# Retention followed by a gated MLP on one core: zero products planned by recent stream, four ranks shifted, and another order of loads and tiles

## The chip, the core and the metric

The kernel runs on one core of a Trainium2 chip. The metric is the device time of one execution in microseconds; before the change it is 212.71 us, the median of three runs (212.57 to 212.76). The engines are named as in the profile: PE (TensorE), DVE (VectorE), ACT (ScalarE), POOL (GpSimd) and SP, whose queue issues the loads. [...]

## What is computed

```python
for t in range(S):                                   # 4 batches, 8 heads, S = 768, D = 64
    state = gamma * state + einsum('bhd,bhe->bhde', k[t], v[t])
    y[t] = einsum('bhd,bhde->bhe', q[t], state) / sqrt(D)
x = y transposed to (B, S, 512)
gate = sigmoid(causal depthwise convolution of x with conv_w, 5 taps)
out = (gate * (x @ w_val)) @ w_out                   # both weights 512 x 512, float32
```

## The kernel before

**Chunks.** The sequence is cut into 6 chunks of 128 tokens for each of 4 batches: 24 chunks g, the four batches of a sequence chunk behind each other. For each chunk TensorE makes scores (k against q), multiplies them by a mask on DVE into `u`, adds k-by-v products to a running state `z_ps` (copied out by ACT as `snap`), and makes y from `u` and from the state before. DVE moves y out of PSUM times a decay (`evac`, L510) into `x`. The first four chunks have no state before them: `first_scores` (L370), `first_mask` (L402), `first_y` (L447) and `first_state` (L414) do them; POOL's `decay` (L346) scales v or k before the state products.

**The MLP.** When all four batches of a sequence chunk are there, ACT rounds x to `xh` (`round_x`, L520), POOL makes the rest `xl` (`rest_x`, L525), and a value tile takes 12 products of 512 columns (`val`, L616: wvh by xh, wvl by xh, wvh by xl). The gate takes one tap on ACT (L599), four on DVE (L601) and a sigmoid (L608); `gated` (L631, DVE) multiplies the two, ACT rounds the product (L638), POOL makes its rest (`rest_gv`, L642), and an output tile takes 12 products (`outp`, L650), a copy by ACT (L660) and a store. There are 24 value tiles and 24 output tiles. The weights arrive as 64-bit floats and each quarter is converted: two ACT passes (L550, L569), two DVE passes (L554, L560), a POOL sum (L573), an ACT rounding (L583) and a POOL rest (L587).

**The order** of every engine's instructions comes from `plan`, a list scheduler that runs when the program is built. Each step has a due time, given by the string `WORK`: `p` the table of positions, `s`, `y`, `z` scores, y and state of the next of the first four chunks, `h` the scores and half state of the first later chunk, `v` the attention of the next later chunk, `w` load and conversion of the next quarter of w_out, `V` a value tile with its gate, `O` an output tile. A backward pass turns due times into ranks; the engine that is free first takes, of its steps whose inputs are there by the planner's own table of durations, the one with the lowest rank. The tuple `LOADS` sets the due times of the first transfers on SP's queue: `q`, `v`, `k` of a chunk's parts (q with transposed k, v, natural k), `a` the first three quarters of a chunk at once, `t` the table `small` (masks, decays), `w` a quarter of w_val.

**Zero products.** While the first value tile has not begun, `plan` puts products of zeros (`filler`, L679) into TensorE's planned rests, so that its clock is held up. Before the change a rest of given length gets `FILLED`, 0.55, of its length in fillers of 0.46 us, whatever ran earlier.

In what follows s0 to s3, y0 to y3 and z0 to z3 are scores, y and state of the first four chunks; a1 to a3 and k1 to k3 their transfers; w0 to w3 the quarters of w_val; V1 the first value tile, O1 the first output tile.

## Time and profile before

| what | before |
|---|---|
| median of 3 runs | 212.71 us |
| the profiled execution, its own time | 214.2 us |
| its span, first to last instruction | 212.4 us |
| PE busy | 200.8 us, 95% |
| DVE, ACT, POOL busy | 123.7, 110.2, 105.7 us |
| mean granted TensorE clock | 0.991 |
| moved by DMA | 36.25 MB |

The span is one execution; 1.8 us of its own time lies outside it. A row of the timeline gives the start and length of a group of instructions, the engine, the line of the kernel, what it writes and reads, how many it holds, and in brackets how long the engine was idle before it and which event ended that. The table by windows gives for each stretch the busy time of the engines, the mean granted clock of TensorE, the share of the DMA engines and the rate in GB/s.

### The profile page before, as it was taken

The page shows a single profiled execution, that of the slowest core. Times are in us where ns is not written, and L with a number is a line of the kernel's source. Part 1 is how long each engine was busy: PE and PEld are TensorE (multiplying, and loading weights), DVE is VectorE, ACT ScalarE, POOL GpSimd, SP SyncE. Part 2 cuts the span into 40 slices and gives each one's busy share as a digit, 9 for nine tenths or more (in the row PEclk, how much of TensorE's full clock was granted, in tenths as well). Part 3 has the DMA queues.
Part 4 walks back from the last instruction along what each step waited for, and adds up shares of the span by engine and source line. Part 5 has one row for each costly group of instructions (what it writes and reads, how often), then busy time and mean ns, then how long its engine had stood idle before and what let it go on. Part 6 is the DMA issues. An engine that isn't in the chain of part 4 may idle for free.

```text
span 212.4 us, 7838 instructions
## 1 busy us (share of the span) xinstructions
PE 200.8 (95%) x3502; PEld 159.9 (75%) x3502; DVE 123.7 (58%) x189; ACT 110.2 (52%) x237; POOL 105.7 (50%) x93
## 2 busy tenths in 40 slices
PE   8648899899999999999999999999999999999992
PEld 3437777678878888788887888788787688878782
DVE  0456999982189922899228992226796269911100
ACT  2655868793568344675447655146364445423221
POOL 0158999999942682535736424626142352204200
PEclk9996999999999999999999999999999999999999
DMA  5999997627575506717476137448111100120122
GB/s 166 367 416 416 360 345 329 201 56 288 176 285 201 204 0 243 257 32 243 179 245 207 49 73 275 153 143 299 62 49 52 52 3 0 70 81 1 48 99 102
DMA packets 9254, 36.25 MB, mean 171 GB/s; under 512 B 1154, under 2 KB 1538, under 8 KB 6660
## 3 DMA queue, kind: packets, MB, share of 16 engines
q1 hardware_dynamic: 5472, 29.43, 39.0%
q10 hardware_dynamic: 3748, 6.32, 8.0%
q8 instruction: 27, 0.44, 0.9%
q14 instruction: 7, 0.06, 0.1%
HBM read 29.46 MB, written 6.29 MB: 168 GB/s over the span
## 4 chain that ended last, share of the span: by engine, by line
PE 77%; DVE 7%; ACT 2%; DMA 1%; issue 1%; DVEq 0%; ACTq 0%
PE mm L650 32%; PE mm L616 27%; PE sy L430 11%; PE sy L357 4%; DVE acc L601 4%; PE z_ps L414 4%; DMA out_dram<-o_sb 1%; DVE top L560 1%; DVE gate L631 1%; DVE acc L554 1%; ACT gate L608 1%; ACT o_sb L660 0%; ACT acc L599 0%; ACT acc L550 0%; DVE x L510 0%
## 5 line engine op out<-in xcount | busy, mean ns | idle before, releaser
L601 DVE SCALAR_TENSOR_TENSOR acc<-x,cw_sb,acc 128x512 f32<-128x512 f32 x96 | 66.8, 750 | 2.8 <-ACT acc L599 2.3
L525 POOL TENSOR_TENSOR xl<-x,xh 128x512 fp32r<-128x512 f32 x24 | 30.8, 1285 | 40.9 <-ACT xh L520 40.8
L642 POOL TENSOR_TENSOR gvl<-gate,gvh 128x512 fp32r<-128x512 f32 x24 | 31.0, 1291 | 31.5 <-ACT gvh L638 31.5
L650 PE MATMUL mm<-woh,gvl 128*128 128x512 f32 (+1 forms) x100 | 38.8, 396 | 0.0
L650 PE MATMUL mm<-woh,gvh 128*128 128x512 f32 (+1 forms) x100 | 38.5, 392 | 0.1
L650 PE MATMUL mm<-wol,gvh 128*128 128x512 f32 (+1 forms) x100 | 37.9, 387 | 0.0
L616 PE MATMUL mm<-xl,wvh 128*128 128x512 f32 x96 | 34.5, 399 | 0.0
L346 POOL TENSOR_TENSOR att<-att,small_sb 128x512 f32<-128x512 f32 x24 | 25.0, 1045 | 15.5 <-DMA att<-in_att_dram 15.5
L616 PE MATMUL mm<-xh,wvh 128*128 128x512 f32 x96 | 32.0, 399 | 0.0
L631 DVE TENSOR_TENSOR gate<-mm,gate 128x512 f32<-128x512 f32 x24 | 16.5, 688 | 20.1 <-PE mm L616 17.8
L616 PE MATMUL mm<-xh,wvl 128*128 128x512 f32 x96 | 27.0, 397 | 0.0
L379 DVE TENSOR_TENSOR u<-sy,small_sb 128x512 f32<-128x512 f32 x20 | 13.7, 687 | 21.5 <-PE sy L357 21.5
L638 ACT CAST gvh<-gate 128x512 fp32r<-128x512 f32 x24 | 14.8, 619 | 21.8 <-DVE gate L631 21.8
L660 ACT COPY o_sb<-mm 128x512 f32<-128x512 f32 (+1 forms) x25 | 14.2, 569 | 18.6 <-PE mm L650 17.4
L510 DVE TENSOR_TENSOR x<-sy,dec 128x512 f32<-128x512 f32 x20 | 13.7, 684 | 17.4 <-PE sy L357 15.3
L650 PEld LDWEIGHTS mm<-woh,gvh 128*128 128x128 f32 x100 | 18.8, 188 | 5.2 <-issue 0.6
L520 ACT CAST xh<-x 128x512 fp32r<-128x512 f32 x24 | 14.8, 618 | 14.2 <-DVE x L510 13.3
L650 PEld LDWEIGHTS mm<-woh,gvl 128*128 128x128 f32 x100 | 18.6, 188 | 4.7 <-POOL gvl L642 0.7
L608 ACT ACTIVATE gate<-acc 128x512 f32<-128x512 f32 x24 | 14.4, 599 | 13.9 <-DVE acc L601 7.6
L650 PEld LDWEIGHTS mm<-wol,gvh 128*128 128x128 f32 x100 | 18.7, 188 | 3.8
L616 PEld LDWEIGHTS mm<-xl,wvh 128*128 128x128 f32 x96 | 18.0, 188 | 4.4
L616 PEld LDWEIGHTS mm<-xh,wvl 128*128 128x128 f32 x96 | 17.9, 188 | 4.3
(51 smaller groups left out, 249.5 us busy)
## 6 DMA issues: line engine op xcount, KB each, us to landing
att<-in_att_dram SPq DMA_DIRECT2D x20, 1024.0 KB, 5.4
out_dram<-o_sb ACTq DMA_DIRECT2D x23, 256.0 KB, 2.0
wst<-in_w_dram SPq DMA_DIRECT2D x8, 512.0 KB, 9.3
att<-in_att_dram SPq DMA_DIRECT2D x3, 768.0 KB, 9.5
att<-in_att_dram SPq DMA_DIRECT2D x5, 256.0 KB, 12.0
att<-in_att_dram SPq DMA_DIRECT2D x1, 512.0 KB, 4.2
out_dram<-o_sb ACTq DMA_DIRECT2D x2, 128.0 KB, 1.7
small_sb<-in_small_dram SPq DMA_DIRECT2D x1, 68.0 KB, 4.2
```

Source lines behind the costliest of these rows:

```text
L346: nc.gpsimd.tensor_tensor(v, v, vd_sb[:, c, :].unsqueeze(2).broadcast_to([P, 8, HALF]), op=ALU.mult)
L430: nc.tensor.matmul(sy[cols, h, off:off + HALF], lhsT=lhsT, rhs=rhs, start=start, stop=True, skip_group_check=True,)
L520: nc.scalar.copy(xh[n][:, :, b], xs[n][:, :, b, HALO:])
L525: nc.gpsimd.tensor_tensor(xl[n][:, :, b], xs[n][:, :, b, HALO:], xh[n][:, :, b].bitcast(F32), op=ALU.subtract)
L601: nc.vector.scalar_tensor_tensor(acc, x[:, :, k:k + P], cw_sb[:, m, k:k + 1], acc, op0=ALU.mult, op1=ALU.add,)
L608: nc.scalar.activation(gate[n, m], accs.pop((n, m)), AF.Sigmoid)
L616: nc.tensor.matmul(vps[n, m], lhsT=w[:, m, ct * P:(ct + 1) * P], rhs=xx[n][:, ct].rearrange("p b t -> p (b t)"), start=(i == 0), stop=(i = ...
L631: nc.vector.tensor_tensor(gv, vps.pop((n, m)), gv, op=ALU.mult)
L638: nc.scalar.copy(gvs[n, m][0], gate[n, m])
L642: engine.tensor_tensor(gvl, gate.pop((n, m)), gvh.bitcast(F32), op=ALU.subtract)
L650: nc.tensor.matmul(ops[n, b, cs.start][:, 0:cs.stop - cs.start], lhsT=gg[:, b * P:(b + 1) * P], rhs=w[:, ct, cs], start=(i == 0), stop=(i ...
L660: nc.scalar.copy(o_sb[:, 0:step], ops.pop((n, b, cs.start))[:, 0:step])
```

## The change

Fillers are planned by another rule. `plan` keeps a list of what TensorE has streamed (`streamed`: 1024 for a filler, 512 for a large product, 32 for each small one, 48 in the first scores and y). In front of each TensorE step with a rest before it, it sums what began in the last `WINDOW`, 3.41 us, and adds as many fillers as lack to `FLOOR`, 4400, at most 0.85 of the rest. Four steps get another rank after the backward pass: `rest_x` of chunk 0, batch 0, `rest_gv` of tile (0, 2) and the first sigmoid (which loads ACT's table) later, `evac` of chunk 2 earlier. The first transfers and the tiles come in another order: a2 is moved ahead of w1, k1 ahead of w1, and k2 and k3 ahead of a3, and the table `small` behind v; in `WORK` the states and attention steps stand earlier among the first tiles, w_out's quarters are spread, and the string ends in five output tiles instead of four.

```diff
-FILL, FILLED = 0.46, 0.55
+FILL, FILLED = 0.46, 0.85
+WINDOW, FLOOR = 3.41, 4400
+LATER = {
+    ("rest_x", 0, 0): 4.98,
+    ("rest_gv", 0, 2): 2.53,
+    ("first_sigmoid",): 1.59,
+    ("evac", 2): -0.60,
+}
@@ in plan, behind the backward pass
+    for s in steps:
+        s.rank += LATER.get((s.fn.__name__, *(a for a in s.args if isinstance(a, int))), 0.0)
@@
+    streamed = []
@@ ahead of a TensorE step
-            for i in range(int((start - since) * FILLED / FILL) if filling else 0):
+            done_lately = sum(w for t, w in streamed if t > start - WINDOW)
+            wanted = max(0, ceil((FLOOR - done_lately) / (2 * P * 4)))
+            for i in range(min(wanted, int((start - since) * FILLED / FILL)) if filling else 0):
                 f = Step(0, "PE", FILL, [], [], filler, (ring,))
...
+                streamed.append((f.start, 2 * P * 4))
...
         if e == "PE":
+            streamed.append((start, 32 * s.small * s.wide + 512 * s.big))
...
-    LOADS = (("q", 0), ("t", 0), ("k", 0), ("v", 0), ("w", 0), ("a", 1), ("w", 1), ("a", 2), ("a", 3), ("k", 1), ("w", 2), ("k", 2), ("k", 3), ("w", 3))
+    LOADS = (("q", 0), ("k", 0), ("v", 0), ("t", 0), ("w", 0), ("a", 1), ("a", 2), ("k", 1), ("w", 1), ("k", 2), ("k", 3), ("a", 3), ("w", 2), ("w", 3))
...
-        "spysysszyyzzzVwwVwwhvVVOOvvOvOVvVvVVOvOvVVO"
-        "vvVOvVvOVVOvOvVVOvvOVOvVOOvvvVVOVOOVVOVOOOO"
+        "spsysyysyzwzzVwhzVVwvvwVOvOOvvOVvVvVVOvOVvV"
+        "vVVvOOvOOVVvOVvOvVOvOVvVVOVOvvvVOVOVVOVOOOOO"
```

## The prediction

> **What bounds the kernel now.** I began with the page: its span, TensorE's busy time, the clock by slices, and the chain of work that ended last.

> ```profile
> span 212.4 us, 7838 instructions
> PE 200.8 (95%) x3502; PEld 159.9 (75%) x3502; DVE 123.7 (58%) x189; ACT 110.2 (52%) x237; POOL 105.7 (50%) x93
> PEclk9996999999999999999999999999999999999999
> PE 77%; DVE 7%; ACT 2%; DMA 1%; issue 1%; DVEq 0%; ACTq 0%
> ```

> TensorE is the bound on the whole, but an average hides where it isn't. The table by windows shows that.

> ```profile
> 10.00:15.00 5.00, 2.63 (x68) 1.83 (x67) 2.77 (x6) 2.59 (x8) 2.67 (x3) 1.00 1.02 418
> 15.00:20.00 5.00, 3.60 (x70) 2.81 (x74) 2.90 (x4) 3.04 (x7) 3.21 (x3) 0.73 1.05 415
> 20.00:25.00 5.00, 4.17 (x110) 3.73 (x104) 4.58 (x7) 3.53 (x7) 5.00 (x6) 0.93 0.96 369
> 25.00:35.00 10.00, 10.00 (x146) 7.77 (x145) 9.92 (x16) 7.63 (x16) 10.00 (x9) 1.00 0.98 374
> 35.00:45.00 10.00, 9.45 (x236) 7.33 (x236) 9.63 (x16) 7.75 (x17) 10.00 (x10) 1.00 0.44 151
> 45.00:206.00 161.00, 160.60 (x2767) 129.80 (x2757) 91.76 (x139) 80.14 (x176) 73.59 (x61) 1.00 0.39 136
> ```

> After the stretch, the columns are busy time of PE, weight loads, DVE, ACT and POOL, then clock, DMA share and GB/s. From 45 to 206 us PE idles 0.40 of 161 us: another order of tiles can win at most that there, and can lose more. From 10 to 25 us the DMA engines are full (0.96 to 1.05) while PE, DVE and POOL have rests: the loads set the pace. From 25 to 45 us PE, DVE and POOL are all nearly full. So the end of the kernel is the moment at which TensorE turns dense, plus the work then left. The timeline of PE shows the moment.

> ```profile
> 11.50 0.90 PE L370 MATMUL sy<-att 64*64 64x128 f32 x32 [1.29 <-DMA att<-in_att_dram]
> ...
> 13.47 0.90 PE L447 MATMUL ye<-u,att 64*64 64x128 f32 x32 [0.45 <-DVE u L402]
> 16.23 0.90 PE L370 MATMUL sy<-att 64*64 64x128 f32 x32 [1.85 <-DMA att<-in_att_dram]
> 17.30 1.22 PE L679 MATMUL ye<-const-float32-0.0 128*128 128x256 f32 x2 [0.17 <-DVE x L510]
> 18.45 1.55 PE L370 MATMUL sy<-att 64*64 64x128 f32 x32
> 19.79 1.27 PE L447 MATMUL ye<-u,att 64*64 64x128 f32 x32
> 21.88 0.90 PE L447 MATMUL ye<-u,att 64*64 64x128 f32 x32 [0.82 <-DVE x L510]
> ...
> 23.35 0.69 PE L414 MATMUL z_ps<-att 64*64 64x64 f32 x32
> 23.98 1.16 PE L679 MATMUL sy<-const-float32-0.0 128*128 128x128 f32 x8
> 25.07 0.69 PE L414 MATMUL z_ps<-att 64*64 64x64 f32 x32
> 25.69 1.20 PE L616 MATMUL mm<-xh,wvh 128*128 128x512 f32 x4
> 26.82 0.69 PE L414 MATMUL z_ps<-att 64*64 64x64 f32 x32
> ```

> These are s1, y1, s2, a filler, s3, y2, y3, z1, fillers, z2, V1 and z3. V1 begins at 25.69; from there on PE is dense, and z3 is still to do. V1 needs the rounded x of all four chunks, the last of which comes of s3.

> **The change, part by part.** *Loads.* For landings I take the engines that waited for them, and the chain from s3 to V1.

> ```profile
> 14.51 0.62 ACT L550 ACTIVATE acc<-wst 128x512 f32<-128x512 f32 x1 [2.41 <-DMA wst<-in_w_dram]
> 20.07 0.65 ACT L550 ACTIVATE acc<-wst 128x512 f32<-128x512 f32 x1 [1.36 <-DMA wst<-in_w_dram]
> 24.48 0.60 ACT L520 CAST xh<-x 128x512 fp32r<-128x512 f32 x1
> ```

> ```profile
> 12.46 0.96 DVE L402 TENSOR_TENSOR u<-sy,xh 128x768 f32<-128x768 f32 x1 [0.65 <-PE sy L370]
> 20.08 0.96 DVE L402 TENSOR_TENSOR u<-sy,xh 128x768 f32<-128x768 f32 x1 [1.92 <-PE sy L370]
> 21.14 0.69 DVE L510 TENSOR_TENSOR x<-ye,base 128x512 f32<-128x512 f32 x1
> ...
> 22.52 0.69 DVE L560 SCALAR_TENSOR_TENSOR top<-wst,acc 128x512 int32<-128x512 int32 x1
> 23.13 0.68 DVE L510 TENSOR_TENSOR x<-ye,base 128x512 f32<-128x512 f32 x1
> ```

> ```profile
> wst<-in_w_dram SPq DMA_DIRECT2D x8, 512.0 KB, 9.3
> att<-in_att_dram SPq DMA_DIRECT2D x3, 768.0 KB, 9.5
> att<-in_att_dram SPq DMA_DIRECT2D x5, 256.0 KB, 12.0
> ```

> w1 lands at 14.51 and w2 at 20.07. Between them come a2, a3, k1 and w2, 768 + 768 + 256 + 512 = 2304 KB (2.36 MB) in 5.56 us, 424 GB/s, which is the rate of the window 15 to 20 (415). So landings go by the sum of bytes ahead. Up to and with w2 the old order carries, behind q0, k0, v0, the table, w0 and a1 (the same in both), w1, a2, a3, k1 and w2: 2816 KB. The new order carries up to and with a3 a2, k1, w1, k2, k3 and a3: 768 + 256 + 512 + 256 + 256 + 768 = 2816 KB. So a3 now lands where w2 did, **20.07**. Before, w1, a2 and a3 make 2048 KB, 512 fewer: 18.8 less the 256 KB of k1, about 18.2, and s3 began at 18.45. The load that V1 waits for is thus late by some 1.8 us: this speaks against the change. a2 moves from 16.23 to about 15.1 (256 KB behind w1's old landing, 0.6 us), k1 to 15.7, k2 and k3 to 17.5 and 18.1, w1 to 16.9.

> *The chain behind a3.* Shortest, by g1's and the last chunk's rows: s to mask 12.46 − 11.50 = 0.96; mask to y 13.47 − 12.46 = 1.01; y 0.90 and a handover of 0.1; evac 0.68; rounding 0.60; handovers 0.15. Sum 4.4: V1 at 24.5. Longest, as before: 25.69 − 18.45 = 7.24, V1 at 27.3. Before, the chain was longer for three reasons in the rows. s3 took 1.55 at a low clock where s2 took 0.90, and DVE idled 1.92 before its mask; y3 waited 0.82 for the evac at 21.14 of y2, which stood behind that mask; and the last evac stood behind w2's conversion (22.52), its rounding behind another ACT pass until 24.48. In the new order y2 has a2 a whole microsecond earlier and a3 later, so its evac is over before s3: the second reason goes. The third stays, as w2 now lands behind a3 and w3 after it: nothing if the queues put evac and rounding first, 0.69 on DVE plus 0.65 on ACT if not. I take 0.6, near the middle. V1 at **25.1**, 0.6 us earlier, bounds 24.5 and 27.3.

> *States.* With k1 to k3 landed by 18.1 and one decay each on POOL, z1, z2 and z3 fit into the rests in which PE waits for a3. z1 and z2 lay ahead of V1 before, z3 behind: its 27.44 − 26.82, **0.62 us**, leaves the dense part. Upper price of not doing so: 0.62, should POOL's decays stand behind other work.

> *Fillers.* The clock by windows (PE busy, clock, DMA, GB/s):

> ```profile
> 13.00:17.00 4.00, 1.70 (x65) 1.00 1.01 404
> 17.00:18.00 1.00, 0.83 (x12) 0.63 1.05 395
> 18.00:19.00 1.00, 1.00 (x14) 0.50 1.07 420
> 19.00:20.00 1.00, 1.00 (x32) 0.50 1.09 446
> 20.00:21.00 1.00, 1.00 (x34) 0.67 1.03 426
> ```

> The clock halves from about 17.4 to 20.7: (0.37 + 0.5 + 0.5 + 0.33) / 0.5 = 3.4 us. Price on the chain: s3's 1.55 − 0.90 = 0.65, with y2's 1.27 − 0.90 at most 1.02. In the planner's own units the 3.4 us before 17.3 held s2's 1536 and about half of y1's 1536, 2300; the new floor is 4400. With 0.85 of a rest to fill, two fillers go where none or one went, and at full count the floor is held. The gain is already in the 4.4 us, which uses warm rows. The fillers themselves cost nothing while PE waits for a3; where data come sooner than planned, one filler (1.16/2 = 0.58) delays a step, bound 0.58. I take nothing, as the trace shows data late: w1 landed 3.0 us after a1's 11.50 with 512 KB, where the planner's 2.7 us per MB makes it 1.4.

> [...]

> *Ranks.* `first_sigmoid` has ACT to itself before any data are there; nothing. `rest_x` (0, 0) and `rest_gv` (0, 2) later let POOL do decays and conversions first, `evac` of chunk 2 earlier serves the chain above. No row prices them apart; bounds ±0.3, half of a DVE evac of 0.68 either way; I take nothing.

> *Supply after V1.* DVE is at 9.92 and 9.63 of 10 us, POOL at 10.00 twice, so PE can only be dense sooner if they deliver sooner, or if PE has work that needs less of them. DVE's last evac and w3 end hardly sooner. But `WORK` now has one more attention step ahead of O1, and three decays leave POOL's full stretch for the one with 2.67 and 3.21 of 5 us busy. I take a loss of 0.1, bounds 0 and 1.2 (all of it).

> *The rest of the string.* The largest possible gain is the 0.40 idle of 45 to 206; a loss has the 0.55 of idle in 10 us from 35 to 45 as its nearest row, and two such stretches, 1.1, are my bound. I take nothing.

> Sum: −0.6 − 0.62 + 0.1 = −1.1 us. The profiled execution took 214.2 us with a span of 212.4, 1.8 outside; it stands 1.5 above the median of 212.71. The sum is a difference within the span, so I subtract it from the median: **211.6 us**.

> **The rivals.**
> *Late a3 (slower).* The mechanism is the chain from s3 to V1 behind a3's landing of 20.07, with evac and rounding queued behind the conversions of w2 and w3. It decides when the chain takes more than 25.69 + 0.62 − 20.07 = 6.2 us. For it: before, it took 7.24, with w2's conversion in it. Against it: 0.65 of that was the clock, and 0.82 the late evac. At 6.6 to 7.24 V1 begins at 26.7 to 27.3, +0.35 to +1.0 with z3 gone: about 213.3.
> *Supply (no change).* DVE and POOL set the time of O1, and PE turns dense sooner only to rest later, between 35 and 45. For: their rows above; DVE gets a3 1.8 us later. Against: the added attention step, 0.69 of mask and 0.68 of evac on DVE for two us of PE. The 1.1 shrinks to about 0.2: 212.5.
> *The clock falls anyway (the change does not do what it says).* The floor is planned on planned starts, and loads land later than planned, so the real density is lower. Price 0.65 of the sum: 212.2. [...] Against: twice the fillers and the states now lie in the rests before s3.

> **How the numbers follow.** My forecast has 0.53, late a3 0.21, supply 0.17, the clock 0.09. The forecast's own range is 210.5 (V1 at 24.5 and 0.4 won later) to 212.2. I take 210.4 to 213.4 for eight in ten, which reaches to the slower case. About 0.2% (0.43 us) is what a measurement of this kernel can tell from none. Faster: 0.52 of the forecast and half of the clock case, 0.56; same: supply, the other half, 0.22; slower 0.22.

> **What would show it.** Right: s3 near 20.1, three states between 16 and 20, no window under 0.95 from 10 to 25 us, V1 near 25.1 with no state behind it before the next attention step, PE above 9.4 of 10 from 35 to 45. Wrong: V1 later than 26.3; a rest on PE with a DVE or POOL releaser between V1 and the first output tiles that grows by what V1 won; more than 0.9 idle from 45 to the end of PE's work; a tail other than the 6.4 us from 206.0 on.

## The result, and the profile after

| | before | changed |
|---|---|---|
| median of 16 runs each | 212.68 us | 214.16 us |
| ratio, 95% interval | | 1.0063 [1.0043, 1.0084] |
| the profiled execution, its own time and span | 214.2 and 212.4 us | 215.84 and 214.0 us |
| mean granted clock of it | 0.991 | 0.984 |

The changed kernel is slower by 0.6%, where 0.5% faster was forecast; 214.16 lies outside the range of 210.4 to 213.4. Beside other kernels in a later job the same file gave 1.0008 [0.9980, 1.0036], so the loss is not the same everywhere. From here on, the few slow runs, more than 1.5% above the fastest of the same kernel, are left out of ratios, counts and medians. The kernel before then has a median of 212.86 us in the 121 runs beside the experiments, and the changed one 213.66 in its 24; the two sets come from different jobs, so that their difference is no measure of the change.

The second line of the new `WORK` reads `vVVvOOvOOVvVOVvOvVOvOVvVOVOvvvVOVOVVOVOOOOO` in the kernel; the diff above prints it with a V too many and a v out of place.

Two stages differ. The first is the head. The table by windows of the profile after (TensorE alone: busy time, clock, DMA share, GB/s):

```profile
16.00:17.00 1.00, 0.66 (x37) 1.00 0.98 399
17.00:18.00 1.00, 0.59 (x32) 0.80 1.00 406
18.00:19.00 1.00, 0.48 (x8) 0.50 1.04 422
...
23.00:24.00 1.00, 1.00 (x22) 0.50 1.10 447
24.00:25.00 1.00, 1.00 (x32) 0.79 1.04 430
```

The clock was meant to hold, and is down from about 17.6 to 24.4, 6.8 us, twice the 3.4 of the execution before. The timeline of PE in the same profile shows what lies before and in it.

```profile
14.10 0.34 PE L432 MATMUL z_ps<-att 64*64 64x64 f32 x7
16.34 0.58 PE L432 MATMUL z_ps<-att 64*64 64x64 f32 x25 [1.91 <-issue]
16.74 0.85 PE L465 MATMUL ye<-u,att 64*64 64x128 f32 x32
18.52 1.56 PE L388 MATMUL sy<-att 64*64 64x128 f32 x32 [0.93 <-DMA att<-in_att_dram]
20.01 2.07 PE L697 MATMUL ye<-const-float32-0.0 128*128 128x256 f32 x4
22.01 1.56 PE L465 MATMUL ye<-u,att 64*64 64x128 f32 x32
23.50 1.14 PE L697 MATMUL sy<-const-float32-0.0 128*128 128x128 f32 x4
24.57 0.69 PE L432 MATMUL z_ps<-att 64*64 64x64 f32 x32
25.80 1.20 PE L634 MATMUL mm<-xh,wvh 128*128 128x512 f32 x4 [0.53 <-ACT xh L538]
```

z1 stops after 7 of 32 products and rests 1.91 us with "issue", nothing that the profile shows. Behind it the clock falls; s3 takes 1.56 us, two fillers 2.07, y3 1.56. V1 begins at 25.80. z2 is still at 24.57, z3 behind V1.

The second is the stretch from 45 us on, by windows of all engines (columns as before the change):

```profile
45.00:60.00 15.00, 14.61 (x417) 11.83 (x417) 7.40 (x13) 8.61 (x20) 13.79 (x12) 1.00 0.53 186
60.00:70.00 10.00, 8.17 (x153) 6.29 (x152) 7.36 (x11) 6.60 (x16) 3.75 (x4) 1.00 0.48 166
70.00:206.00 136.00, 135.54 (x2130) 109.52 (x2130) 76.68 (x117) 63.53 (x137) 55.92 (x46) 1.00 0.33 120
```

PE idles 2.68 of these 161 us, 1.83 of them from 60 to 70. The timelines of ACT and PE name the reason: an output copy waits for a free buffer, that is for a store (8.4 us to landing, the longest of those from 30 to 90 us; 4.6 before the change). PE waits 1.10 us for that copy, and 0.73 for `turned`, a later step of ACT, which worked without a rest from the copy up to it.

```profile
62.40 0.58 ACT L678 COPY o_sb<-mm 128x512 f32<-128x512 f32 x1 [3.34 <-DMA out_dram<-o_sb]
```

```profile
63.03 0.50 PE L634 MATMUL mm<-xh,wvh 128*128 128x512 f32 x1 [1.10 <-ACT o_sb L678]
68.39 0.69 PE L448 MATMUL sy<-att,snap 64*64 64x64 f32 x32 [0.73 <-ACT turned L498]
```

### The profile page after: what moved, and what is told of

Its sections match the earlier page's. It is cut to its first block, busy times and chain, and to the rows that moved or that the text cites. A ratio compares the mean times of both kernels' runs of the same rounds, so it can differ in the third digit from the quotient of the medians.

```text
span 214.0 us, 7830 instructions
## 1 busy us (share of the span) xinstructions
PE 202.4 (95%) x3498; PEld 160.9 (75%) x3498; DVE 124.1 (58%) x189; ACT 109.4 (51%) x237; POOL 106.0 (50%) x93
## 4 chain that ended last, share of the span: by engine, by line
PE 67%; POOL 7%; ACT 5%; DMA 5%; DVE 2%; issue 1%; ACTq 0%
PE mm L668 27%; PE mm L634 26%; PE sy L448 8%; DMA out_dram<-o_sb 5%; PE sy L375 3%; POOL top L591 2%; PE z_ps L432 2%; DVE acc L619 2%; POOL gvl L660 2%; POOL wol L605 2%; ACT o_sb L678 1%; ACT gate L626 1%; POOL att L364 1%; ACT dec L515 1%; POOL wvl L605 1%
## 5 line engine op out<-in xcount | busy, mean ns | idle before, releaser
L668 PE MATMUL mm<-woh,gvl 128*128 128x512 f32 (+1 forms) x100 | 38.0, 389 | 0.0
L634 PE MATMUL mm<-xh,wvh 128*128 128x512 f32 x96 | 32.7, 400 | 1.6 <-ACT o_sb L678 1.1
L397 DVE TENSOR_TENSOR u<-sy,small_sb 128x512 f32<-128x512 f32 x20 | 13.7, 687 | 23.4 <-PE sy L375 20.8
L649 DVE TENSOR_TENSOR gate<-mm,gate 128x512 f32<-128x512 f32 x24 | 16.5, 686 | 15.3 <-PE mm L634 15.1
L656 ACT CAST gvh<-gate 128x512 fp32r<-128x512 f32 x24 | 14.9, 620 | 17.5 <-DVE gate L649 17.3
L634 PEld LDWEIGHTS mm<-xh,wvh 128*128 128x128 f32 x96 | 17.7, 188 | 6.1 <-ACT o_sb L678 1.5
## 6 DMA issues: line engine op xcount, KB each, us to landing
out_dram<-o_sb ACTq DMA_DIRECT2D x23, 256.0 KB, 2.1
wst<-in_w_dram SPq DMA_DIRECT2D x8, 512.0 KB, 8.8
att<-in_att_dram SPq DMA_DIRECT2D x3, 768.0 KB, 7.3
att<-in_att_dram SPq DMA_DIRECT2D x5, 256.0 KB, 7.5
att<-in_att_dram SPq DMA_DIRECT2D x1, 512.0 KB, 4.1
```

What stands on the lines that cost most here:

```text
L397: nc.vector.tensor_tensor(us[g], sy[:, :, 0:256].rearrange("p x (a t) -> p x a t", t=HALF), tri_sb.unsqueeze(1).unsqueeze(1).broadcast_to( ...
L634: nc.tensor.matmul(vps[n, m], lhsT=w[:, m, ct * P:(ct + 1) * P], rhs=xx[n][:, ct].rearrange("p b t -> p (b t)"), start=(i == 0), stop=(i = ...
L649: nc.vector.tensor_tensor(gv, vps.pop((n, m)), gv, op=ALU.mult)
L656: nc.scalar.copy(gvs[n, m][0], gate[n, m])
L668: nc.tensor.matmul(ops[n, b, cs.start][:, 0:cs.stop - cs.start], lhsT=gg[:, b * P:(b + 1) * P], rhs=w[:, ct, cs], start=(i == 0), stop=(i ...
```

## The experiments

Every run carries its mean granted clock. Where the whole run is at full clock it is 1.0; a drop to half clock as long as the 3.4 us of the execution before costs some 0.008, an estimate (1.7 of 212 us). I count runs at 0.995 or more as held. Each kernel was timed beside the kernel before, in four jobs, each on one chip; that kernel's median was 212.74, 212.80, 213.52 and 212.76 us there, so ratios are compared across jobs, and times within one. A ratio is the one on record with its interval, not the quotient of the medians shown (for changed_again, 1.0008 against 1.0030). Most intervals reach 0.003 to either side, so that a smaller difference can't be told from none.

| run | median, us | ratio to before, 95% interval | held runs: median | others: median |
|---|---|---|---|---|
| kernel before, four jobs | 212.86 | 1 | 85 of 121: 212.64 | 36: 213.97 |
| changed, both jobs | 213.66 | 1.0063, 1.0008 | 5 of 24: 213.21 | 19: 213.69 |
| four_store_buffers | 213.21 | 1.0002 [0.9973, 1.0032] | 1 of 12: 211.49 | 11: 213.23 |
| old_tile_order | 220.07 | 1.0333 [1.0279, 1.0388] | 1 of 6: 218.34 | 5: 220.09 |
| old_filler_rule | 213.15 | 1.0028 [0.9997, 1.0060] | 0 of 12 | 12: 213.16 |
| only_filler_rule | 212.80 | 1.0000 [0.9968, 1.0032] | 8 of 12: 212.63 | 4: 213.87 |
| before_four_buffers | 212.09 | 0.9961 [0.9931, 0.9991] | 10 of 11: 212.06 | 1: 213.66 |
| table_first | 212.57 | 0.9979 [0.9948, 1.0010] | 7 of 12: 212.18 | 5: 213.24 |
| zeros_in_fetch | 213.71 | 1.0036 [1.0012, 1.0060] | 4 of 12: 212.99 | 8: 214.12 |
| table_first_and_zeros | 214.18 | 1.0056 [1.0029, 1.0082] | 10 of 12: 214.03 | 2: 214.93 |
| a3_before_states | 212.50 | 0.9960 [0.9929, 0.9991] | 7 of 12: 212.34 | 5: 213.22 |
| old_loads | 213.58 | 1.0014 [0.9989, 1.0039] | 9 of 11: 213.47 | 2: 214.69 |
| new_loads_only | 220.61 | 1.0313 [1.0255, 1.0372] | 0 of 4 | 4: 220.61 |
| a3_before_k1 | 218.37 | 1.0231 [1.0198, 1.0263] | 0 of 6 | 6: 218.37 |
| changed_again | 213.41 | 1.0008 [0.9980, 1.0036] | 2 of 10: 211.65 | 8: 213.48 |
| changed_table_first | 214.57 | 1.0054 [1.0027, 1.0081] | 4 of 12: 214.67 | 8: 214.32 |
| changed_four_buffers | 213.14 | 0.9999 [0.9973, 1.0026] | 1 of 11: 211.28 | 10: 213.19 |
| changed_both | 212.61 | 0.9993 [0.9961, 1.0025] | 4 of 12: 212.38 | 8: 213.12 |

**Stores, and parts undone.** After the result two theories stood, stores and head. The first edit gives the output copies more room and leaves all orders as planned; the others undo one part.

```diff
 four_store_buffers, before_four_buffers, changed_four_buffers
-        o_sb = mlp.tile([P, 512], F32, name="o_sb")
+        o_sb = mlp.tile([P, 512], F32, name="o_sb", bufs=4)
 old_tile_order: the changed kernel with the old WORK
 old_filler_rule: the changed kernel with
-            for i in range(min(wanted, int((start - since) * FILLED / FILL)) if filling else 0):
+            for i in range(int((start - since) * FILLED / FILL) if filling else 0):
-FILL, FILLED = 0.46, 0.85
+FILL, FILLED = 0.46, 0.55
 only_filler_rule: the kernel before with the new rule, FILLED 0.85
```

> The changed kernel with four buffers for the output copies instead of two; the planned order of every engine is untouched. Theory S (stores): in the profile after, ACT waits 3.34 us at 62.40 for a store that took 8.4 us among loads, and PE idles about 1.8 us between 60 and 70. With a buffer free ACT doesn't wait: no rest on PE with the copy's line as releaser, time lower by 1.0 to 1.8 us, about 212.7. Theory H (head): the loss lies before V1, in the longer drop of the clock and the fetch of instructions; then the time stays within 0.4 us of the changed kernel's 214.2.

> The changed kernel with the old string WORK; fillers, ranks and loads stay new. Theory S: the attention steps no longer bunch ahead of the first stores, so the 1.8 us of rest between 60 and 70 goes, about 212.5 to 212.9. Theory H: the head keeps its low clock and its 1.9 us rest for instructions, so 213.8 or more.

> The changed kernel with the old rule for fillers (0.55 of each rest, no window); ranks, loads and tiles stay new. Theory H: three fillers fewer in the head, of which the pair at 20.01 took 2.07 us at half clock and held y3 back by 0.8: 0.5 to 1.0 us less, unless the clock drops for longer without them, which would add 0.6. Theory S: within 0.4 us of the changed kernel, as the stores' wait is untouched.

> The kernel before with the new rule for fillers alone. My prediction's price for a warm head is 0.65 us: 212.0 if the new rule holds the clock. Theory H, that planned fillers land in rests whose data come late and so don't hold the clock, says 212.5 to 213.2, with slices of low clock left between 15 and 25 us. Theory S says nothing of it, as no store is moved: 212.7 or less.

With four buffers the rest from 60 to 70 is gone from the profile of four_store_buffers:

```profile
60.00:70.00 10.00, 10.00 (x163) 7.98 (x161) 9.89 (x16) 6.45 (x16) 3.73 (x4) 1.00 0.63 224
```

The ratio fell from 1.0063 to 1.0002, by 1.3 us, within the 1.0 to 1.8 that theory S expected, though the two are from different jobs. old_tile_order fits neither theory: the old string with the new loads costs 3.3%, and PE idles 4.7 us from 25 to 60 us in its profile, most of it for the rounded x of V1 (1.6) and for POOL's part of w_out (1.3). The ratio of old_filler_rule lies 0.0035, some 0.75 us, below that of the changed kernel, within the 0.5 to 1.0 that H expected, but not one of its 12 runs held the clock, so the new rule is not what loses it. Its tiles past 35 us are also ordered otherwise, since fillers enter the planner's count of instructions, and it has no rest from 55 to 75; what the difference is made of was not separated. only_filler_rule is a clean miss for the price in my prediction: the rule alone does nothing to the old order, 1.0000, and no more runs hold the clock (8 of 12, against 85 of 121). Its 212.80 lies where theory H had it, but the profile taken, of a run that held the clock, shows none of H's slices of low clock.

**The control, the late table, and more zeros.** The table small lands late now, and DVE's masks and POOL's first decay wait for it (7.23 us, against 5.36 before). In the profile of four_store_buffers the clock is at 0.72 from 10 to 15 us, right behind. The next kernels start from four buffers.

```diff
 table_first, changed_both: four_store_buffers with; changed_table_first: the changed kernel with
-    LOADS = (("q", 0), ("k", 0), ("v", 0), ("t", 0), ("w", 0), ...
+    LOADS = (("q", 0), ("t", 0), ("k", 0), ("v", 0), ("w", 0), ...
 zeros_in_fetch: four_store_buffers with; table_first_and_zeros: table_first with
+EXTRA = {("first_state", 1): ("sc", "sc"), ("first_scores", 3): ("sc", "sc")}
...
+            for r in EXTRA.get((s.fn.__name__, *(a for a in s.args if isinstance(a, int))), ()):
+                f = Step(0, "PE", FILL, [], [], filler, (r,))
+                f.start = f.end = f.free = start
+                order.append(f)
```

> The kernel before with four buffers for the output copies, orders untouched; the control for the same edit of the changed kernel. Theory S: in the profile before, no store took over 4.6 us and ACT waited for none between 45 and 206 us, so nothing is won: within 0.4 us of 212.7. If it gains 0.5 us or more, the wait for stores is not what the change brought.

> The changed kernel with four buffers, and with the table small loaded second, as before the change; only the place of one to three fillers around z0 moves with it. Theory C (clock): the late table holds z0 until 9.9 in the run with four buffers, and the clock dropped right behind that rest; with the table early z0 runs by 8.2 and fewer runs drop: mean clock of the runs from 0.991 to above 0.993, time from 213.2 to about 212.7. Rival F (fetch): the drop hangs on the 1.9 us rest for instructions in z1 alone; clock and time stay as they are within 0.3.

> The changed kernel with four buffers, and two more fillers each ahead of z1 and of s3, all else in order as it is. Theory F: about 1 us of products lies in the rest for instructions, and the clock holds behind it: most runs at 0.995 or more, 212.0 to 212.4. Theory C (late table): drops stay, 213.2 within 0.4. If fillers cost more than they bring (they use up instructions), 213.6 or more.

> Both of the last two edits. If both rests let the clock fall, only this one has nearly all runs at 0.995 or more, and its time is that of the one run of four_store_buffers at clock 1.0, 211.5 to 211.9, under the kernel before by about 1 us, which is the gain forecast for the head. If the clock is not what costs, it stays at 212.7 or more.

The control went against theory S: the kernel before gains 0.39% of the same edit, where the changed one gained 0.61%, across two jobs. A part of this gain is common to both kernels and lies in the tail, past the 206 us up to which the expectation had looked. With two buffers the last output copy waits for an earlier store, to have its buffer; with four it waits for TensorE alone. ACT in the profiles of the kernel before and of before_four_buffers:

```profile
208.90 0.37 ACT L660 COPY o_sb<-mm 128x256 f32<-128x256 f32 x1 [1.02 <-DMA out_dram<-o_sb]
...
206.85 0.37 ACT L660 COPY o_sb<-mm 128x256 f32<-128x256 f32 x1 [0.57 <-PE mm L650]
```

The last product begins at 208.13 and at 206.53, so that the copy follows it by 0.77 us with two buffers and by 0.32 with four; in the changed kernel it is 0.56 and 0.32. So in these profiles 0.45 and 0.24 us of the gains are the tail's; what made the rest of the 0.39% was not found. That the change loses by waiting for stores isn't shown by its gain from four buffers, though that wait made the 1.83 us of the execution shown.

table_first bore theory C out as to the clock: 7 of 12 runs hold it, and 11 of 24 with changed_both, against 2 of 23 with the table late and four buffers. What it gains in time, 0.0023, lies within the intervals. zeros_in_fetch came out as the last case of its expectation, fillers that cost more than they bring: 213.71. With both edits 10 of 12 runs hold the clock, yet the time is 1.6 us above table_first, where 211.5 to 211.9 was expected. The timeline of PE from the fillers ahead of s3 to V1, in a profile of one of the two runs that don't hold it (215.56 us; its clock falls behind 25 us):

```profile
19.17 1.16 PE L704 MATMUL sy<-const-float32-0.0 128*128 128x128 f32 x8
20.26 0.90 PE L395 MATMUL sy<-att 64*64 64x128 f32 x32
21.09 1.14 PE L704 MATMUL ye<-const-float32-0.0 128*128 128x256 f32 x4
22.23 0.76 PE L472 MATMUL ye<-u,att 64*64 64x128 f32 x19
24.05 0.45 PE L472 MATMUL ye<-u,att 64*64 64x64 f32 x13 [1.05 <-issue]
...
26.70 2.07 PE L641 MATMUL mm<-xh,wvh 128*128 128x512 f32 x4 [0.94 <-ACT xh L545]
```

and that of table_first:

```profile
16.87 0.58 PE L432 MATMUL z_ps<-att 64*64 64x64 f32 x25 [1.69 <-issue]
17.27 0.85 PE L465 MATMUL ye<-u,att 64*64 64x128 f32 x32
19.18 0.90 PE L388 MATMUL sy<-att 64*64 64x128 f32 x32 [1.06 <-DMA att<-in_att_dram]
20.01 1.14 PE L697 MATMUL ye<-const-float32-0.0 128*128 128x256 f32 x4
21.16 0.90 PE L465 MATMUL ye<-u,att 64*64 64x128 f32 x32
21.99 0.60 PE L697 MATMUL sy<-const-float32-0.0 128*128 128x128 f32 x3
23.06 0.27 PE L697 MATMUL sy<-const-float32-0.0 128*128 128x128 f32 x1 [0.48 <-issue]
...
24.66 0.50 PE L634 MATMUL mm<-xh,wvh 128*128 128x512 f32 x1 [0.70 <-ACT xh L538]
```

Between the two rests of table_first lie 25 + 32 + 32 + 4 + 32 + 3 = 128 products, each with its load of weights. The rest comes with the count of products, not with data. This holds beyond the two profiles: in the first 40 us of all 18, TensorE rests with "issue" 23 times, and each time 221 or 222, 349 or 350, or 603 products after the program's start, whatever stands there: steps of 128, but for one or two products. (Only zeros_in_fetch has no such rest.) With sixteen more filler products ahead, the second one moves out of the fillers, where it cost nothing, into y3 (20.26 begins s3, 22.23 y3), on which V1 hangs. This rest of 1.05 us is about half of the 2.04 by which V1 comes later than in table_first. The other half is there before: s3 begins 1.08 us later, behind the added fillers of 19.17, where in table_first it had waited for a3 until 19.18.

**Which load, which string.** For what was left over before_four_buffers (1.0020 against it, by the ratios 0.9979 and 0.9961) I moved a3, and took loads and tiles apart.

```diff
 a3_before_states: table_first with
+    LOADS = q0 t0 k0 v0 w0 a1 a2 k1 w1 a3 k2 k3 w2 w3
 a3_before_k1: table_first with
+    LOADS = q0 t0 k0 v0 w0 a1 a2 a3 k1 w1 k2 k3 w2 w3
 old_loads: four_store_buffers with the old LOADS
 new_loads_only: before_four_buffers with the new LOADS
```

> The kernel of table_first (changed, four buffers, table second) with a3 loaded ahead of k2 and k3 instead of behind them; the orders of the other engines differ in a handful of rows. Theory A (late a3): in table_first s3 began at 19.18 after a wait of 1.06 us for a3, V1 at 24.66, where in before_four_buffers s3 began at 16.58 and V1 at 24.04. With 512 KB less ahead of it, 1.3 us at 410 GB/s, s3 begins near 18 and V1 near 23.6: 211.6 to 212.1 from 212.57. Rival W: V1 waits for ACT, which rounds behind the conversions of w2 and w3, so V1 and the time stay within 0.3.

> The changed kernel (new fillers, ranks, tiles) with four buffers and the old LOADS in full. Theory A: what is left between table_first and before_four_buffers, 0.45 us, is the loads' order: 211.8 to 212.2. Rival T (tiles): it is the string WORK, and the time stays at 212.6 or more.

> The kernel before with four buffers and the new LOADS alone; old tiles, fillers and ranks. Theory A: the late table and the late a3 cost what they cost in the changed kernel, 0.8 to 1.3 us over before_four_buffers: 212.9 to 213.4. Rival T: the old string needs its loads (old_tile_order took 220), so 215 or more, and the two edits can't be priced one by one.

> The kernel of table_first with a2 and a3 right behind a1 and the states' k1 to k3 behind w1. Theory A: a3 another 0.77 MB earlier than in a3_before_states, s3 near 16.5 as before the change, V1 at 23 to 23.5: 211.3 to 211.8, under before_four_buffers. Rival: z1 to z3 now come behind V1 and w1's conversion holds the value tiles, 212.3 or more.

a3_before_states has 0.9960, 0.0019 under table_first and inside both intervals: theory A's 0.5 to 1.0 us can't be told from nothing. Its profile speaks for the mechanism of rival W. s3 no longer waits for a3 and begins at 18.74 (z1 rests 1.95 us with "issue" ahead of it), but V1 at 25.48, later than the 24.66 of table_first: DVE is done with the last evac at 23.27, and ACT, busy with conversions and a tap of the gate, rounds only at 24.83.

```profile
22.59 0.68 DVE L528 TENSOR_TENSOR x<-ye,base 128x512 f32<-128x512 f32 x1
24.83 0.60 ACT L538 CAST xh<-x 128x512 fp32r<-128x512 f32 x1
```

old_loads is worse than table_first, by 0.35%, and new_loads_only and a3_before_k1 cost 2 to 3%: theory A falls for them, and rival T holds in both runs for which it was stated. The planner's order for every engine follows the loads: the old string with the new loads is 3% slower in both kernels that had it, the new string with the old loads hardly. So the parts of this change can't be priced one by one. In a3_before_k1 the rests with "issue" lie in y2 (1.07 us) and y3 (1.18).

**Both edits on one chip.** What stayed open was how much of the loss is the stores' and how much the table's.

> The changed kernel as it is, beside the next three on one chip. Its ratio to the kernel before was 1.0063; both theories expect 1.004 to 1.008 again, with most runs at a clock under 0.995.

> The changed kernel with the table small loaded second, two buffers for the output copies. Theory C (the late table lets the clock fall): over half of the runs at 0.995 or more, ratio lower than the changed kernel's by 0.002 to 0.004, about 1.003. Rival S (stores alone): ratio within 0.0015 of the changed kernel's.

> The changed kernel with four buffers, beside the other three. Theory S: 0.004 to 0.006 below the changed kernel's ratio, clocks as low as its; if only the chips differed between the earlier jobs, within 0.0015 of it.

> Both edits, the kernel of table_first once more. If the two causes are apart, their gains add: 0.007 to 0.009 below the changed kernel's ratio, 0.996 to 0.999 of the kernel before. If one hides the other, no better than the better of the two.

The changed kernel came out at 1.0008 here, so little was left to divide. changed_table_first got worse, 1.0054: theory C misses. changed_four_buffers lies 0.0009 below it, where theory S had 0.004 to 0.006, and changed_both 0.0015, where 0.007 to 0.009 was expected. In the profile of changed_table_first ACT waits 2.9 us for a store and PE idles 1.36 us from 55 to 75; in that of changed_again 0.8 and nothing. Whether an output copy waits for one of the first stores changes with the head, and between the two profiles of the changed kernel; with four buffers none does in the profiles of changed_four_buffers and changed_both. With four buffers the table first brings 0.0006 to 0.0023. The two causes don't add; how the 0.63% splits stays open.

## Why the prediction was wrong

**The chain behind a3: the step that failed.** I put 5.0 us from a3 to V1, the shortest chain of 4.4 and 0.6 for the queues of DVE and ACT. From s3 to V1 it took 25.80 − 18.52 = 7.28 in the profile shown, 24.84 − 18.34 = 6.50 in changed_again, and 24.66 − 19.18 = 5.48 in table_first at full clock. In the profile shown, the low clock makes 2.2 of the excess: 0.67 in s3, 0.66 in y3, and 0.85 by which the fillers behind s3, 2.07 us long, hold y3 back. In changed_again, where the clock is full by then, the queues make it, DVE and ACT:

```profile
21.30 0.70 DVE L572 TENSOR_SCALAR acc<-acc 128x512 int32<-128x512 int32 x1 [1.04 <-ACT acc L568]
22.09 0.69 DVE L578 SCALAR_TENSOR_TENSOR top<-wst,acc 128x512 int32<-128x512 int32 x1
22.70 0.68 DVE L528 TENSOR_TENSOR x<-ye,base 128x512 f32<-128x512 f32 x1
...
23.41 0.69 ACT L617 ACTIVATE acc<-x,cw_sb 128x512 f32<-128x512 f32 x1
24.04 0.23 ACT L522 COPY x<-x 128x64 f32<-128x64 f32 x1
24.18 0.61 ACT L538 CAST xh<-x 128x512 fp32r<-128x512 f32 x1
```

y3 (20.38, 0.90 long) is done at 21.28, and the last evac begins 1.4 us later, behind two passes of a conversion. It is done at 23.38, and the rounding begins 0.8 us later, behind a tap of the gate and a copy. The same tap and copy stand ahead of the last rounding in the profile shown and in table_first. This was the third of my reasons, which I let stay at 0.6.

**The base of the difference: a second error.** "The sum is a difference within the span, so I subtract it from the median." The execution that I read took 214.2 us, where 85 of 121 runs hold the clock and have a median of 212.64. I saw the 1.5 us between the two and didn't ask which of the rows they came from. The profile of before_four_buffers, whose orders are those of the kernel before, is a run without the drop (clock 0.998, span 210.4); PE, and ACT at the landing of w2:

```profile
14.57 0.90 PE L370 MATMUL sy<-att 64*64 64x128 f32 x32 [0.41 <-DMA att<-in_att_dram]
...
16.58 0.90 PE L370 MATMUL sy<-att 64*64 64x128 f32 x32 [0.47 <-DVE u L402]
17.27 0.88 PE L447 MATMUL ye<-u,att 64*64 64x128 f32 x32
19.15 0.90 PE L447 MATMUL ye<-u,att 64*64 64x128 f32 x32 [1.00 <-DVE x L510]
...
24.04 1.20 PE L616 MATMUL mm<-xh,wvh 128*128 128x512 f32 x4
...
18.42 0.64 ACT L550 ACTIVATE acc<-wst 128x512 f32<-128x512 f32 x1 [1.59 <-DMA wst<-in_w_dram]
```

V1 begins at 24.04, not 25.69. The rows that make the difference are the loads: a2 landed at 14.57 and not 16.23, w2 at 18.42 and not 20.07, each some 1.65 us sooner, like V1, and a2 before the clock fell at 17.3 in the execution read. only_filler_rule, with two buffers, has w2 at 18.48 and V1 at 24.07. Why the loads of the execution read were late isn't known.

**a3, and luck.** On this base my rule, that a3 lands where w2 did, was right: 18.42 by the rule, 18.52 measured. s3 had begun at 16.58, behind DVE and not behind a3, so a3 came at least 1.9 us later than before, as forecast. That my 25.1 for V1 came near the 25.80 and 24.84 of the changed kernel is luck: the landing was taken 1.5 us too late and the chain 1.5 to 2.3 too short. The base alone is not what failed: with the rows of before_four_buffers my terms give V1 at 18.42 + 5.0 = 23.4, again 0.6 ahead of 24.04. Measured, V1 lost 0.8 us (changed_again) and 1.8 (the profile shown). (Of the loads, "2048 KB, 512 fewer" should be 768 fewer than 2816; the 18.2 takes all of it off and stands.)

**What the loss is, in profiles.** Against only_filler_rule (the old order with the new rule, two buffers, clock 0.998), the span of changed_again is 0.8 us longer (211.6 against 210.8), as V1 is (24.84 against 24.07); from V1 to the end both have 186.7 or 186.8. In the profile shown V1 makes 1.7 of 3.2 us, and the end is 188.2 behind it, with the rests from 60 to 70. These are single executions.

**States.** 0.62 us were counted and didn't come. z1 alone moved ahead of s3; z2 stands at 24.57 and z3 behind V1, by the planner's order.

**Clock.** I took it as held. The rival "the clock falls anyway", with 0.09, came true as to the clock: 19 of 24 runs fall, where 36 of 121 did before. It did not come true as to the time, for which it had 212.2. Runs with a drop are 1.3 us longer in the kernel before (213.97 − 212.64) and 1.0 or 0.7 with four buffers and the table first (213.24 and 213.12 against 212.18 and 212.38), but 0.5 in the changed kernel (213.69 − 213.21). In its first job, where it lost 0.63%, its three runs that held the clock have a median of 213.70, the eleven others 213.92. So the share of drops doesn't account for that loss. No edit removed the drop alone, and in the execution that I read the loads were late before it; its price stays open. The 0.65 for a warm head was not shown: only_filler_rule, the new fillers in the old order, gave 1.0000. The same program drops in some runs and not in others, so the planned starts alone, which the new rule counts, don't decide it.

**The rest of the string.** Taken as nothing, with a bound of 1.1 us; in the execution shown PE idles 2.68 us from 45 to 206 instead of 0.40, in that of changed_again 0.84.

**Supply.** The small term was right in the profile shown: PE is busy 10.00 of 10 us from 35 to 45, and the 0.53 that it idles from 25 to 35 is its wait ahead of V1. **Late a3 (slower)** had the right sign, and its chain was over the 6.2 us from which it decides in both profiles of the changed kernel. In changed_again (6.50) its mechanism is the one at work, a conversion ahead of the evac and ACT's queue ahead of the rounding; in the profile shown (7.28) it is the low clock for the most part.

The fastest against the kernel before are before_four_buffers, in the old order, and a3_before_states, in the new one: 0.9961 and 0.9960, which can't be told apart. No version with the new order was shown to beat the old order with four buffers.

## What to carry to other kernels

Before a sum is taken off a median, ask whether the execution that was read is a typical one: compare its time and its clock with the other runs, and find the rows that make up the difference. Check a forecast by its terms and not by its end: a landing too late and a chain too short gave a V1 that looked right. For the last step on which the dense part hangs, write down what stands ahead of it in each engine's queue. A filler is not free where TensorE rests by the count of products, here in steps of 128: sixteen filler products more moved a rest of 1.05 us onto V1's chain. Count the products up to the next rest before adding any. Give a change's control the same edit: four buffers looked like the cause until the kernel before gained from them too.

## What the runs showed of the hardware

A store of 256 KB lands in 2.1 us at the median of the changed kernel, and took 8.4 among the loads of later chunks (DMA share 0.76 to 0.95 from 56 to 62 us), long enough to block ACT, and PE behind it, through a ring of two buffers.
